# A fused attention and two-layer MoE kernel: the next-to-last gates issued ahead of the last products with v, and the last routing chain cut into other portions

## The chip, the cores and the metric

The kernel runs on one core of one Trainium2 chip, as one program. The metric is the device time of one execution in microseconds (us), taken as the median of several executions.

## The reference

Three stages follow each other. `attn_out` feeds the first MoE layer, whose result `x` feeds the second.

```python
mask = q_assign[:, :, :, None] == k_assign[:, :, None, :]   # same nearest centroid
attn = softmax(where(mask, scale * q @ k.T, -1e9)) @ v      # 2 batches, 8 heads, 768, 64
x = attn_out.transpose(0, 2, 1, 3).reshape(1536, 512)

logits = x @ w_gate                                         # layer 1: 8 experts
e = argmax(logits); gate = softmax(logits)[e]
y[i] = gate * relu(x[i] @ w1[e]) @ w2[e]                    # first `capacity` tokens of an expert

# layer 2: the same without capacity, times sigmoid(x @ w_output_gate)[e]
```

Each token goes to one expert. To know which token is in which place of which expert, a prefix count over all 1536 tokens is needed, so the full routing of layer 1 is known only after the last token has left attention.

## The kernel before, in words

**Attention.** The work is 8 pairs of heads (`pi` 0 to 7; two batches, four pairs each), and in each pair 12 steps (6 blocks of 128 queries, 2 heads). A step is: scores on TensorE (L238), row maximum on VectorE (L246), exponential on ScalarE (L254), and two steps later six transposes (L268) with evictions (L270). A "half" is three query blocks, 384 tokens; when a half of a pair is transposed, its products with v (`av`, 24 matmuls, L280) are issued and `av_out` copies them out on ScalarE (L287). `fin(pi, hf)` then calls `norm`: three matmuls `px` on TensorE turn the result back to tokens and give the partial gate logits (L299), VectorE takes reciprocals `ri` of the softmax sums (L301, L302), multiplies the logits into `lp` (L307), adds them up in `lg_sb` (L312, L313) and scales the rows of x (L315; by chunk L317 in the last half). All order of issue is written out by hand: each engine takes its instructions in the order in which this code emits them.

**Routing of a half.** After the fourth pair of a batch a half of tokens is complete, and the generator `after_half(b, hf, rows)` routes it: `choose` (five VectorE steps, L522 to L533), `sums` (three absolute sums of the last 128 columns on ScalarE, `jk`, L1430), `exps` (L1452 to L1454), `before` (running counts, L1436), `power` (a power of two to scale the rows by, L1441 and L669 to L673), `scale` (the rows themselves, 512 wide, one instruction per block; L1447 on ScalarE, L1449 on GpSimd), `gates` (L1457 to L1463) and `write` (rows to DRAM, `x1d`, L1467). `turns` issues several such chains round robin; `turns_by(k, ...)` does so k rounds at a time and yields between. The half that ends a batch goes on with `positions` (two matmuls, L1522), `places`, `load_order`, `taken`, and `invert`, which builds one-hot tables (`av` L587, `rv` L595) and multiplies them (`pinv`, L600). From that `select` makes the list of rows of an expert (L646, L649), and `gather` fetches them by indirect DMA on GpSimd (L867).

**The seam.** The last iteration of attention's loop (i = 97) calls, in this order, `fin(7, 0)`, both portions of `av(7, 1)` and `av_out(7, 1)`. `fin(7, 0)` only appends the steps of `after_half(1, 0)` to a list `bg`, which is emptied one step per iteration and fully after the loop; so those steps stand behind the last `av_out` in every queue. What is left, `norm` and `after_half` of half (7, 1), is the generator `last()`, handed to the MoE as a task.

**The head unit.** `M.run` works through units (one to three tiles of rows of one expert). Unit 0, the head, has 128 rows of an expert that the first batch already fixed, so it can run before the last routing is known. Per unit there are eight steps f of `mm1` (12 matmuls, L930; evicted by ScalarE `hh`, L932, then VectorE `hl`, L933) and four steps d of `mm2` (24 matmuls, L996; copied out by L998). `mm1` and `mm2` share one PSUM pool `ps_mm` of three buffers: a step can start only when the step three before it has been evicted. `SA` says how many portions of the routing task are issued ahead of each of the head's 12 steps, in the order f0 to f7, d0 to d3. Unit 1 begins with transposes `pxt` (L907) of gathered rows, which wait for the last routing. Weights of later units come over SyncE's queue (L791, L793), are split into two 16-bit parts by ScalarE (L820) and VectorE (L827), and multiplied three times.

Of the kernel before, what the change touches and what calls it, by code (L numbers as in the profile page):

```python
# [8 lines left out]
F32 = mybir.dt.float32  # L9
# [19 lines left out]
def attention(tc, end, ps_t, ident, wu, q, k, v, centroids, wg, x_half, lg_sb, consts, before_half, after_half, extra, slot):  # L29
# [13 lines left out]
    with ExitStack() as ctx:  # L43
# [239 lines left out]
        def av_out(pi, hf):  # L283
# [3 lines left out]
            nc.scalar.copy(ot, d["av", hf][:, :W])  # L287
            d["avo", hf] = ot

        def norm(pi, hf, by_chunk=False):  # L290
            b, hp = pairs[pi]
            d = st[pi]
            ot = d["avo", hf]
            c0 = hf * HALF
            t0 = b * C + c0
            px = ps_t.tile([P, 512], F32, tag="t", name="px")
            pv = px[:, :HALF * (P + 2 * E)].rearrange("p (c m) -> p c m", c=HALF)
            for c in range(HALF):
                nc.tensor.matmul(pv[:, c, :], ot[:, c * P:(c + 1) * P], rw[:, hp, :], start=True, stop=True)  # L299
            ri = end.tile([P, HALF, 2], F32, tag="ri", name="ri", bufs=2)  # L300
            nc.vector.tensor_scalar_add(ri, d["sm"][:, c0:c0 + HALF, :], 1e-9)  # L301
            nc.vector.reciprocal(ri, ri)  # L302
            rib = lambda n: ri.unsqueeze(3).to_broadcast([P, HALF, 2, n])
            xo = x_half(b, hf)[:, :, hp * P:(hp + 1) * P].rearrange("p c (j d) -> p c j d", j=2)
            lp = end.tile([P, HALF, 2, E], F32, tag="lp", name="lp", bufs=2)
            lo = lg_sb[:, t0:t0 + HALF, :]
            nc.vector.tensor_tensor(lp, pv[:, :, P:].rearrange("p c (j e) -> p c j e", j=2), rib(E), op=ALU.mult)  # L307
            if hp == 0:
                nc.gpsimd.tensor_tensor(lo, lp[:, :, 0], lp[:, :, 1], op=ALU.add)
            else:  # L310
                e = nc.vector if hp == NP - 1 else nc.gpsimd
                e.tensor_tensor(lo, lo, lp[:, :, 0], op=ALU.add)  # L312
                e.tensor_tensor(lo, lo, lp[:, :, 1], op=ALU.add)  # L313
            if not by_chunk:
                nc.vector.tensor_tensor(xo, pv[:, :, :P].rearrange("p c (j d) -> p c j d", j=2), rib(D), op=ALU.mult)  # L315
                return
            return [lambda c=c: nc.vector.tensor_tensor(xo[:, c], pv[:, c, :P].rearrange("p (j d) -> p j d", j=2),  # L317
                                                        ri[:, c].unsqueeze(2).to_broadcast([P, 2, D]), op=ALU.mult)
                    for c in range(HALF)]

        def fin(pi, hf):
            b, hp = pairs[pi]
            norm(pi, hf)
            if hp == NP - 2:
                bg.extend(before_half(b, hf))
            if hp == NP - 1:
                g = after_half(b, hf, ())
                bg.extend([lambda: next(g, None)] * (24 if hf else 8))

        def last():  # L330
            rows = norm(NPR - 1, 1, True)
# [142 lines left out]
def turns_by(k, *chains):  # L474

    chains = list(chains)
    while chains:
        for _ in range(k):
            chains = [c for c in chains if next(c, c) is not c]
        if chains:  # L480
            yield
# [225 lines left out]
class MoE:  # L707
# [23 lines left out]
    FX = 1  # L731
    FB = 2
    FY = 7
    SA = (1, 0, 1, 0, 1, 1, 0, 1, 1, 0, 1, 1)
    SB = (1, 3, 2, 1, 1, 1, 1, 1, 1, 1, 1, 1)
    Q = 2

# [539 lines left out]
def tile_kernel(tc, q, k, v, centroids, wg1, w11, w12, cap_in, wg2, wog2, w21, w22, out,  # L1277
# [15 lines left out]
    with ExitStack() as ctx:  # L1293
# [27 lines left out]
        if True:  # L1321
# [87 lines left out]
            def after_half(b, hf, rows):  # L1409
# [33 lines left out]
                    yield from R.power(rp, am, sx, rx)  # L1443

                def scale(i):
                    if end and i == 0:
                        nc.scalar.mul(x[:, i, :DM], x[:, i, :DM], sx[:, i:i + 1])  # L1447
                    else:
                        nc.gpsimd.tensor_scalar(x[:, i, :DM], x[:, i, :DM], sx[:, i:i + 1], None, op0=ALU.mult)  # L1449
# [72 lines left out]
                        nc.tensor.matmul(pp[:, i * E:(i + 1) * E], R.to[:, i], rs, start=True, stop=True)  # L1522
                    return pp

                yield from turns_by(1000 if end else 3, R.choose(rp, lg, None, oh1[:, t], mx), sums())
                if last:
                    rs = rp.tile([P, E], F16, tag="rs", name="rs")
                    with nc.allow_low_precision("whole numbers"):
# [2 lines left out]
                    vc = small("vc", C)  # L1531
                    lohi, ro = [], []
                if end:
                    yield
                    pp = positions()
                    exps()
                    yield from turns_by(KS, before(), power(), shift())
                    for i in range(HALF):
                        scale(i)
                    yield from turns_by(KS, places(), gates(), load_order())  # L1540
                    for i in range(HALF):
                        write(nc.scalar, slice(i, i + 1))
                    turns(taken())
                else:
                    yield
                    exps()
                    yield from turns_by(3, before(), power())
                    yield
                    for i in range(HALF):
                        scale(i)  # L1550
                    yield from turns_by(3, gates())
                    write(nc.sync, slice(0, HALF))
                    if not last:
                        return
                    yield
                    pp = positions()
                    yield from turns_by(3, places(), load_order())
                    yield from turns_by(3, taken())
# [343 lines left out]
```

## Time and profile before

| | |
|---|---|
| runs shown | 629.02, 629.38, 632.44 us; median 629.38 us |
| the profiled execution | 627.58 us, of which the span from first to last instruction is 625.7 us |
| TensorE (PE) busy | 569.5 us, 91% of the span |
| VectorE (DVE), ScalarE (ACT), GpSimd (POOL) busy | 467.1, 419.9, 212.8 us |
| mean granted TensorE clock | 0.976 of full speed |
| attention, head unit, rest of the MoE | to about 275, to 293, to 626 us |

Times on the trace are counted from the start of the span. A bracket at the end of a timeline row gives how long the engine had stood idle before that instruction and who ended the wait. PEclk is the granted clock of TensorE: 1.00 is 2.4 GHz, 0.50 is 1.2 GHz, and a value between them is a stretch with some of each. "ACTq" is a DMA issued from ScalarE's queue. A matmul's length in a row includes its way through the array, so lengths of following rows overlap; the distance between starts is the better measure.

### The profile page before, as it was taken

The page shows a single profiled execution, that of the slowest core. Times are in us where ns is not written, and L with a number is a line of the kernel's source. Part 1 is how long each engine was busy: PE and PEld are TensorE (multiplying, and loading weights), DVE is VectorE, ACT ScalarE, POOL GpSimd, SP SyncE. Part 2 cuts the span into 40 slices and gives each one's busy share as a digit, 9 for nine tenths or more (in the row PEclk, how much of TensorE's full clock was granted, in tenths as well). Part 3 has the DMA queues.
Part 4 walks back from the last instruction along what each step waited for, and adds up shares of the span by engine and source line. Part 5 has one row for each costly group of instructions (what it writes and reads, how often), then busy time and mean ns, then how long its engine had stood idle before and what let it go on. Part 6 is the DMA issues. An engine that isn't in the chain of part 4 may idle for free.

```text
span 625.7 us, 14519 instructions
## 1 busy us (share of the span) xinstructions
PE 569.5 (91%) x5430; PEld 470.8 (75%) x5430; DVE 467.1 (75%) x1219; ACT 419.9 (67%) x885; POOL 212.8 (34%) x420
## 2 busy tenths in 40 slices
PE   6899999998999988958999998998788899999992
PEld 2766767675767666637878997997767888999992
DVE  5767777679899677756597689788776566989881
ACT  4766666776666669832676776876654466979781
POOL 8702020204150210134615268344333623253341
PEclk9899999999999999998899999999899799999998
DMA  5779391826429952314486776977754457998930
GB/s 148 212 231 275 97 216 46 210 60 151 141 89 233 252 171 82 133 56 138 130 269 204 243 244 179 304 238 244 248 181 152 164 174 238 305 308 298 321 111 20
DMA packets 75518, 117.55 MB, mean 188 GB/s; under 512 B 10504, under 2 KB 43400, under 8 KB 75441
## 3 DMA queue, kind: packets, MB, share of 16 engines
q1 hardware_dynamic: 71585, 105.96, 56.1%
q0 software_dynamic: 3264, 9.72, 4.9%
q8 instruction: 45, 0.74, 0.5%
q10 hardware_dynamic: 592, 0.87, 0.4%
q14 instruction: 32, 0.26, 0.1%
HBM read 84.28 MB, written 12.87 MB: 155 GB/s over the span
## 4 chain that ended last, share of the span: by engine, by line
PE 63%; DVE 16%; ACT 9%; DMA 5%; issue 4%; SPq 1%; POOL 0%; ACTq 0%; DVEq 0%; POOLq 0%
PE ph L930 17%; PE py L996 13%; PE av L280 9%; PE pss L238 7%; PE ppt L268 6%; DVE wl L827 3%; DVE nm L246 3%; PE pz L971 3%; ACT pe L254 2%; PE pyo L1609 2%; PE pxt L907 2%; ACT pt L270 1%; ACT wh L820 1%; DMA xg<-x2d,idx2a 1%; DMA xg<-x2d,idx 1%
## 5 line engine op out<-in xcount | busy, mean ns | idle before, releaser
L827 DVE SCALAR_TENSOR_TENSOR wl<-raw,sw,wh 128x1024 f16<-128x1024 f32 x128 | 163.5, 1283 | 18.5 <-ACT wh L820 18.4
L820 ACT ACTIVATE wh<-raw,sw 128x1024 f16<-128x1024 f32 x128 | 145.7, 1146 | 2.6 <-DMA x<-ot 2.5
L246 DVE TENSOR_REDUCE nm<-pss 128x1 f32<-128x768 f32 x96 | 91.4, 952 | 40.5 <-PE pss L238 36.8
L254 ACT ACTIVATE pe<-pss,nm 128x768 f32<-128x768 f32 x96 | 87.1, 907 | 24.2 <-DVE nm L246 24.2
L930 PEld LDWEIGHTS <-wh 128*128 128x128 f16 x1152 | 91.3, 102 | 14.2 <-issue 9.7
L238 PE MATMUL pss<-y,x 128*128 128x384 f32 x384 | 93.5, 364 | 4.1 <-ACT pe L254 3.2
L268 PE MATMUL ppt<-ident,pe 128*128 128x128 f32 x576 | 80.5, 275 | 3.3 <-ACT pt L270 1.4
L238 PEld LDWEIGHTS pss<-y,x 128*128 128x128 f32 x384 | 63.0, 190 | 24.4 <-issue 12.3
L270 ACT COPY pt<-ppt 128x384 f32<-128x384 f32 x128 | 57.9, 482 | 28.6 <-PE ppt L268 28.2
L268 PEld LDWEIGHTS ppt<-ident,pe 128*128 128x128 f32 x576 | 69.3, 142 | 8.9 <-ACT pt L270 2.3
L930 PE MATMUL ph<-xh,wh 128*128 128x192 f16 (+14 forms) x576 | 69.5, 246 | 6.7 <-DVE hl L933 5.7
L996 PEld LDWEIGHTS <-wh 128*128 128x128 f16 x960 | 72.4, 99 | 3.8 <-issue 0.5
L930 PE MATMUL ph<-xl,wh 128*128 128x192 f16 (+14 forms) x576 | 69.5, 246 | 0.2
L930 PE MATMUL ph<-xh,wl 128*128 128x192 f16 (+14 forms) x576 | 69.5, 246 | 0.0
L280 PE MATMUL av<-pt,v 128*64 128x384 f32 x384 | 68.8, 494 | 0.0
L932 ACT ACTIVATE hh<-ph 128x128 f16<-128x128 f32 (+14 forms) x144 | 44.1, 312 | 35.7 <-PE ph L930 34.3
L933 DVE SCALAR_TENSOR_TENSOR hl<-ph,hh 128x128 f16<-128x128 f32 (+14 forms) x144 | 46.4, 333 | 24.6 <-ACT hh L932 24.0
L930 PEld LDWEIGHTS <-wl 128*128 128x128 f16 x576 | 47.4, 102 | 1.9
L996 PE MATMUL py<-hl,wh 128*128 128x192 f16 (+13 forms) x480 | 46.6, 239 | 0.8 <-DVE hl L933 0.8
L996 PE MATMUL py<-hh,wh 128*128 128x192 f16 (+13 forms) x480 | 46.5, 239 | 0.6 <-DVE hl L933 0.4
L280 PEld LDWEIGHTS av<-pt,v 128*64 128x64 f32 x384 | 24.8, 136 | 28.4 <-issue 28.2
L996 PE MATMUL py<-hh,wl 128*128 128x192 f16 (+13 forms) x480 | 46.1, 239 | 0.0
(319 smaller groups left out, 858.8 us busy)
## 6 DMA issues: line engine op xcount, KB each, us to landing
raw<-in_moe_w SPq DMA_DIRECT2D x64, 1024.0 KB, 5.9
y<-kh SPq DMA_DIRECT2D x31, 192.0 KB, 4.0
x<-qh SPq DMA_DIRECT2D x30, 192.0 KB, 4.2
q<-in_q SPq DMA_DIRECT2D x8, 384.0 KB, 5.1
k<-in_k SPq DMA_DIRECT2D x8, 384.0 KB, 5.3
x<-ql SPq DMA_DIRECT2D x16, 192.0 KB, 3.6
v<-in_v SPq DMA_DIRECT2D x8, 384.0 KB, 4.1
out<-zt SPq DMA_DIRECT2D x1, 3072.0 KB, 11.0
```

What stands on the lines that cost most here:

```text
L238: nc.tensor.matmul(p[:, hf, :W], xx[:, c * P:(c + 1) * P], yy[:, hf * W:(hf + 1) * W], start=a, stop=o)
L246: nc.vector.tensor_reduce(nm, p[:, :, :W], axis=AX.XY, op=ALU.max, negate=True)
L254: nc.scalar.activation(pe, p[:, :, :W], AF.Exp, bias=d["nm", c, j], scale=1.0, accum_out=d["sm"][:, c, j:j + 1])
L268: nc.tensor.transpose(p[:, kc * P:(kc + 1) * P], pe[:, kh, kc * P:(kc + 1) * P], ident)
L270: eng(pt[:, kh * HALF:(kh + 1) * HALF, (c % HALF) * P:(c % HALF + 1) * P], p.rearrange("p (a b) -> p a b", a=HALF))
L280: nc.tensor.matmul(p[j * D:(j + 1) * D, :W], d["v"][:, j, kc, :], d["pt", hf, j][:, kc, :], start=(kc == 0), stop=(kc == C - 1))
L820: nc.scalar.activation(hi[:, :, s], x[:, :, s], AF.Copy, scale=sw)
L827: nc.vector.scalar_tensor_tensor(lo[:, :, s], x[:, :, s], sw, hi[:, :, s], op0=ALU.mult, op1=ALU.subtract, accum_out=fl)
L930: nc.tensor.matmul(p[:, :N], w[:, c, fs], x[:, c, :N], start=(k == 0), stop=(k == 11))
L932: nc.scalar.activation(hh[:, f, :N], p[:, :N], AF.Relu)
L933: nc.vector.scalar_tensor_tensor(hl[:, f, :N], p[:, :N], 0.0, hh[:, f, :N], op0=ALU.max, op1=ALU.subtract)
L996: nc.tensor.matmul(p[:, :N], w[:, f, s], x[:, f, :N], start=(k == 0), stop=(k == 23))
```

## The change

Four things change. (1) When `fin` reaches the last pair (which it does for half 0 only), it empties `bg`, runs `after_half(1, 0)` to its end at once, and issues the reciprocals `ri` of half (7, 1) by the new function `inverse`; all that now stands ahead of the last `av` and `av_out` in the queues. (2) `norm` uses reciprocals that exist already. (3) `SA` is other: one portion ahead of each of f0 to f5, none ahead of f6 to d1, one ahead of d2 and of d3. (4) The chain of the last half is cut into other portions: `choose` and `sums` two rounds at a time instead of all at once; then `exps`, `power`, `before`, `shift` and `scale` in one portion; then a portion with nothing in it; then `positions`, `places`, `gates`, `load_order` and the writes in one; then `taken` and `invert`. Of the three `scale` instructions two are now ScalarE's, one GpSimd's (before: one and two).

Portion by portion (the step of the head unit that it is issued ahead of):

| | before | after |
|---|---|---|
| norm, all of choose and sums, `rs` | f0 | f0, f1, f2 (norm and two rounds; two rounds; the rest) |
| positions | f2 | f4 |
| exps, power, before, shift | f2, f4 | f2 |
| scale | f4 | f2 |
| places, gates, load_order | f4, f5, f7, d0 | f4 |
| writes, taken, invert tables | d0 | f4 (writes), f5 |
| pinv, select, gather | d2 | d2 |

```diff
--- before.py
+++ after.py
@@ -287,6 +287,14 @@
             nc.scalar.copy(ot, d["av", hf][:, :W])
             d["avo", hf] = ot
 
+        def inverse(pi, hf):
+
+            d = st[pi]
+            c0 = hf * HALF
+            ri = d["ri", hf] = end.tile([P, HALF, 2], F32, tag="ri", name="ri", bufs=2)
+            nc.vector.tensor_scalar_add(ri, d["sm"][:, c0:c0 + HALF, :], 1e-9)
+            nc.vector.reciprocal(ri, ri)
+
         def norm(pi, hf, by_chunk=False):
             b, hp = pairs[pi]
             d = st[pi]
@@ -297,9 +305,9 @@
             pv = px[:, :HALF * (P + 2 * E)].rearrange("p (c m) -> p c m", c=HALF)
             for c in range(HALF):
                 nc.tensor.matmul(pv[:, c, :], ot[:, c * P:(c + 1) * P], rw[:, hp, :], start=True, stop=True)
-            ri = end.tile([P, HALF, 2], F32, tag="ri", name="ri", bufs=2)
-            nc.vector.tensor_scalar_add(ri, d["sm"][:, c0:c0 + HALF, :], 1e-9)
-            nc.vector.reciprocal(ri, ri)
+            if ("ri", hf) not in d:
+                inverse(pi, hf)
+            ri = d["ri", hf]
             rib = lambda n: ri.unsqueeze(3).to_broadcast([P, HALF, 2, n])
             xo = x_half(b, hf)[:, :, hp * P:(hp + 1) * P].rearrange("p c (j d) -> p c j d", j=2)
             lp = end.tile([P, HALF, 2, E], F32, tag="lp", name="lp", bufs=2)
@@ -325,7 +333,15 @@
                 bg.extend(before_half(b, hf))
             if hp == NP - 1:
                 g = after_half(b, hf, ())
-                bg.extend([lambda: next(g, None)] * (24 if hf else 8))
+                if pi == NPR - 1:
+
+                    while bg:
+                        bg.pop(0)()
+                    for _ in g:
+                        pass
+                    inverse(pi, 1)
+                else:
+                    bg.extend([lambda: next(g, None)] * (24 if hf else 8))
 
         def last():
             rows = norm(NPR - 1, 1, True)
@@ -731,7 +747,7 @@
     FX = 1
     FB = 2
     FY = 7
-    SA = (1, 0, 1, 0, 1, 1, 0, 1, 1, 0, 1, 1)
+    SA = (1, 1, 1, 1, 1, 1, 0, 0, 0, 0, 1, 1)
     SB = (1, 3, 2, 1, 1, 1, 1, 1, 1, 1, 1, 1)
     Q = 2
 
@@ -1443,7 +1459,7 @@
                     yield from R.power(rp, am, sx, rx)
 
                 def scale(i):
-                    if end and i == 0:
+                    if end and i != 1:
                         nc.scalar.mul(x[:, i, :DM], x[:, i, :DM], sx[:, i:i + 1])
                     else:
                         nc.gpsimd.tensor_scalar(x[:, i, :DM], x[:, i, :DM], sx[:, i:i + 1], None, op0=ALU.mult)
@@ -1522,7 +1538,7 @@
                         nc.tensor.matmul(pp[:, i * E:(i + 1) * E], R.to[:, i], rs, start=True, stop=True)
                     return pp
 
-                yield from turns_by(1000 if end else 3, R.choose(rp, lg, None, oh1[:, t], mx), sums())
+                yield from turns_by(2 if end else 3, R.choose(rp, lg, None, oh1[:, t], mx), sums())
                 if last:
                     rs = rp.tile([P, E], F16, tag="rs", name="rs")
                     with nc.allow_low_precision("whole numbers"):
@@ -1531,15 +1547,17 @@
                     vc = small("vc", C)
                     lohi, ro = [], []
                 if end:
-                    yield
-                    pp = positions()
                     exps()
-                    yield from turns_by(KS, before(), power(), shift())
+                    turns(power(), before(), shift())
                     for i in range(HALF):
                         scale(i)
-                    yield from turns_by(KS, places(), gates(), load_order())
+                    yield
+                    yield
+                    pp = positions()
+                    turns(places(), gates(), load_order())
                     for i in range(HALF):
                         write(nc.scalar, slice(i, i + 1))
+                    yield
                     turns(taken())
                 else:
                     yield
```

## Rows read from the trace of the kernel before

**Rows 1.** The page's part 4: shares of the span on the chain that ended last

```profile
PE 63%; DVE 16%; ACT 9%; DMA 5%; issue 4%; SPq 1%; POOL 0%; ACTq 0%; DVEq 0%; POOLq 0%
```

**Rows 2.** The chain of 264 to 304 us: start, length, what

```profile
290.89 0.18 DVE idx L649
...
292.08 3.12 DMA xg<-x1d,idx
```

**Rows 3.** Timeline, 270 to 279 us: start, length, engine, line, [idle before <- releaser]

```profile
270.12 4.09 PE L280 MATMUL av<-pt,v 128*64 128x384 f32 x24
...
270.84 0.55 DVE L315 TENSOR_TENSOR x<-px,ri 128x384 f32<-128x384 f32 x1
...
274.26 0.48 ACT L287 COPY avo<-av 128x384 f32<-128x384 f32 x1 [4.36 <-PE av L280]
...
274.63 0.31 ACT L1430 ACTIVATE jk<-x 128x128 f16<-128x128 f32 x1
...
274.79 1.00 PE L299 MATMUL px<-rw,avo 128*128 128x144 f32 x6 [0.58 <-ACT avo L287]
...
275.94 0.16 DVE L1441 SCALAR_TENSOR_TENSOR am<-am 128x3 f32<-128x3 f32 x1 [3.32 <-ACT jk L1430]
...
276.69 4.68 POOL L1449 TENSOR_SCALAR x<-x,sx 128x512 f32<-128x512 f32 x3 [4.00 <-DVE sx L671]
...
277.72 0.58 DVE L301 TENSOR_SCALAR ri<-sm 128x6 f32<-128x6 f32 x1
...
278.65 0.21 DVE L307 TENSOR_TENSOR lp<-px,ri 128x48 f32<-128x48 f32 x1
...
278.90 0.18 DVE L312 TENSOR_TENSOR lg_sb<-lg_sb,lp 128x24 f32<-128x24 f32 x1
```

**Rows 4.** Timeline, 279 to 282 us: the last half's choice of experts

```profile
279.71 0.28 DVE L317 TENSOR_TENSOR x<-px,ri 128x128 f32<-128x128 f32 x1
...
279.80 0.31 ACT L1430 ACTIVATE jk<-x 128x128 f16<-128x128 f32 x1 [3.79 <-DVE er L525]
...
279.92 0.61 DVE L527 TENSOR_TENSOR er<-er,rev 128x24 f32<-128x24 f32 x1
...
281.36 0.21 PE L1522 MATMUL ppos<-rs,to 128*128 128x8 f16 x2 [4.22 <-DVE rs L1529]
```

**Rows 5.** Timeline, 282 to 286 us: the head unit beside the routing chain

```profile
282.72 0.28 ACT L932 ACTIVATE hh<-ph 128x128 f16<-128x128 f32 x1 [0.47 <-PE ph L930]
...
283.03 0.29 DVE L933 SCALAR_TENSOR_TENSOR hl<-ph,hh 128x128 f16<-128x128 f32 x1 [0.36 <-ACT hh L932]
...
284.18 0.71 ACT L1447 ACTIVATE x<-x,sx 128x512 f32<-128x512 f32 x1
...
284.60 0.17 DVE L1505 TENSOR_TENSOR pre<-pre,ppos 128x48 f32<-128x48 f32 x1
...
285.84 0.15 DVE L1463 TENSOR_TENSOR x<-rx,sm 128x3 f32<-128x3 f32 x1
```

**Rows 6.** Timeline, 287 to 296 us: from the writes to the next unit

```profile
287.35 1.35 ACTq L1467 DMA_DIRECT2D x1d<-x  x3
...
288.01 0.15 DVE L1511 TENSOR_SCALAR pl<-code 128x6 int32<-128x6 int32 x1
...
289.11 1.02 DVE L595 TENSOR_TENSOR rv<-lo,iota 128x384 f16<-128x384 int32 x2
...
290.27 0.61 PE L996 MATMUL py<-hh,wh 128*128 128x128 f16 x8
...
291.61 0.61 PE L996 MATMUL py<-hh,wh 128*128 128x128 f16 x8
...
295.33 0.66 PE L907 MATMUL pxt<-ident,xg 64*128 64x64 f32 x4 [2.22 <-DMA xg<-x1d,idx]
```

**Rows 7.** Stretches: length, busy us of PE, PEld, DVE, ACT, POOL (instructions), granted clock, DMA

```profile
281.40:285.10 3.70, 3.70 (x39) 3.70 (x40) 2.33 (x19) 1.54 (x5) 2.38 (x3) 0.54 0.56 222
295.30:302.10 6.80, 6.22 (x84) 5.99 (x85) 4.17 (x11) 5.09 (x11) 5.86 (x16) 0.50 0.30 89
455.70:462.50 6.80, 4.11 (x38) 3.38 (x36) 6.26 (x29) 4.94 (x12) 3.14 (x5) 1.00 0.63 211
```

More of the change, by code (lines that the diff above doesn't have):

```diff
@@ L1533, in after_half @@
                 if end:
+                    exps()
+                    turns(power(), before(), shift())
+                    for i in range(HALF):
+                        scale(i)
+                    yield
                     yield
                     pp = positions()
-                    exps()
-                    yield from turns_by(KS, before(), power(), shift())
-                    for i in range(HALF):
-                        scale(i)
-                    yield from turns_by(KS, places(), gates(), load_order())
+                    turns(places(), gates(), load_order())
                     for i in range(HALF):
                         write(nc.scalar, slice(i, i + 1))
+                    yield
                     turns(taken())
```

## The prediction

> **What bounds the kernel now.** I read the chain that ended last first: TensorE holds 63% of the span, VectorE 16% [rows 1]. For this change only the seam between attention and the first layer counts, so next came the chain there: the routing of the last half runs on VectorE until the index of unit 1's rows is out at 291.07 (290.89 + 0.18), the gather starts at 292.08 and lands 3.12 later [rows 2], and the transposes of unit 1, for which TensorE stood idle 2.22, start at 295.33 [rows 6]. What moves that transpose moves the end: behind it TensorE is the bound, and weight splits and loads are issued by the units, so they shift along. Then I read the timeline. ScalarE waits 4.36 for the products with v and only then does its sums `jk`; so VectorE waits 3.32 for them at `am`; so the last half's `lp` comes at 278.65, although its matmuls `px` were issued at 274.79 and took 1.00 [rows 3]. TensorE, after f0 and f1, waits 4.22 at the matmuls of `positions` [rows 4]. The windows show that it pays twice: from 281.4 to 285.1 its clock is 0.54 of full, and from 295.3 to 302.1 it is 0.50 [rows 7].
>
> **Part 1, the next-to-last gates ahead of the last products.** x of that half is ready at 271.4 (270.84 + 0.55). The three `jk` take 1.3 together (274.63 to `am` at 275.94) [rows 3], so `am` moves from 275.94 to 272.7. From `am` to `ri` 1.78 pass, from `ri` to the reciprocals' end 0.9 [rows 3]: all is done at 275.4, inside the products with v (4.09 from 270.12) and `px`. `av_out` is not delayed: ScalarE is free 1.3 before the products end at 274.2; without that margin every microsecond there would be one on `px`. So `lp` starts when `px` ends, about 275.9: **a lead of 2.75**. The write of that half goes to SyncE's queue about 3 earlier; nothing else stands in that queue then, so it neither costs nor gains. GpSimd's three scalings (4.68) move from 276.69 to 273.45, on an idle engine.
>
> **Part 2, choose in three portions.** Before, the whole choice ran ahead of f0's evictions; now f0's and f1's stand inside it. `jk` 0 starts 1.15 after `lp` [rows 3, 4]: 277.05. Behind `jk` 1 (0.43 later) ScalarE does `hh` 0 (0.28) at 277.8, VectorE then `hl` 0 (0.29) [rows 5], and the third step of the choice, which came 1.27 after `lp` [rows 3, 4], starts at 278.3 instead of 277.2. Then a row scaling (0.28 [rows 4]), `jk` 2, `hh` 1 and `hl` 1 lead to 279.65, and the tail of the choice ends at 280.0. Before, `positions` stood at 281.36: the lead is down to 1.3. TensorE waits in pieces now: for `hl` 0 ahead of f3, for the choice ahead of f4.
>
> **Part 3, two scalings on ScalarE.** `exps`, `power` and the counts are nine short VectorE steps about 0.1 apart, as the twelve between 284.60 and 285.84 are [rows 5], and end near 280.8. ScalarE then scales two blocks (0.71 each [rows 5]) ahead of `hh` 2 and `hh` 3, so `hl` 3 ends at 282.8. GpSimd's one scaling less is worth nothing, as GpSimd has no other work until the gather. `places` stands behind `hl` 3: 282.8 instead of 284.60, a lead of 1.8, since before it had waited there for f2 and f3 at the low clock.
>
> **Part 4, places to writes in one portion.** From `places` to the gate took 1.4 with one `hl` between [rows 5]; without it 1.1, to 283.9. The three writes wait for that gate at the head of ScalarE's queue and take 1.35 [rows 6]. Behind them stands `hh` 4, although f4 has long been computed: it ends at 285.5, `hl` 4 at 285.8, and f7, which needs that buffer, starts there. The writes, issued by 285.2 instead of 288.7, land earlier, but the gather waits for the index.
>
> **Part 5, taken and the tables ahead of `hl` 5.** They take 2.12 (288.01 to 289.11 + 1.02) [rows 6], so end at 287.9, and `hl` 5 at 288.2. `mm2`'s d0 reuses the buffer of f5: it starts at **288.2**. Two steps d take 2.68 at full clock (1.34 from 290.27 to 291.61 [rows 6]), and `pinv` stands behind d1: 290.9. Before, d1 was done just as the tables were, and the index started 0.76 after the tables' end; now all six small matmuls come after d1, some 0.2 more. Index at 291.6 to 291.9 instead of 290.89: **the lead of 2.75 is gone, and the gather lands 0.7 later.** I take 0.7; the bounds are 0 (VectorE's steps closer together than I set them) and 1.2 (one more slow step).
>
> **The clock.** By these steps TensorE between 277.6 and 288.2 works some 3.6 (f3 to f7, 0.67 each, half of a step d) and is idle some 7, in pieces of 0.7 to 1.9. No stretch of before has that pattern. Nearest are a fall at 295.3 after the 2.22 idle ahead of it, and a stretch without fall, 455.7 to 462.5, with 4.11 busy of 6.80 [rows 6, 7]. The idle share here is larger than in the second, so I take it that the clock falls to 1.2 GHz, for a stretch as that at 281.4 (3.7). The part of it that lies on waits costs nothing; on d0 and d1 it costs at most another 2.7. I take half, 1.35. In return unit 1's low stretch (6.8, in which at half clock 6.22 of work is worth 3.1) should come out shorter: between nothing and 1.55 back, I take 0.8.
> The Trainium skill ("TensorE: Matmul & The Clock Gate", section "A second HAM failure mode: psum-queue depth-cycling") describes this pattern: short idle pieces between groups, as PSUM buffers cycle, make the clock swing, and throughput suffers. It speaks against this change; by it the sum is this one or that of the second rival, while the stretch at 455.7 disagrees with it.
>
> **Sum.** 0.7 + 1.35 - 0.8 = +1.25 us against the profiled execution's 627.58: 628.8. That execution lies 1.8 under the median of 629.38; so the forecast for the median is **630.6**.
>
> **VectorE beside GpSimd.** While GpSimd scales (276.69 to 281.37), two VectorE steps took 0.58 and 0.61 where their like take 0.18 to 0.21; yet `lg`, with two inputs in SBUF, took 0.18 there [rows 3, 4]. So one step per GpSimd instruction pays some 0.4. After, the scalings lie at 273.45 to 278.1; two of three prices fall ahead of `px`'s end, the third on `lp` to the choice, instead of on its third step: no change.
> The Trainium skill ("SBUF — State Buffer", section "Who interferes with whom") says more: the shared port is held for a whole instruction, and a VectorE instruction with two SBUF inputs waits for it. `lg`'s 0.18 disagrees; what it would do here is the fourth rival.
>
> **The rivals.**
> First, the clock stays at 2.4 GHz through the head: +0.7, unit 1 as before, 630.1. The stretch at 455.7 speaks for it, the larger idle share against it. Chance 0.18.
> Second, **slower**: the clock falls before d0 begins and stays low through d1. It decides if the fall lies between some 284 and 288. Then d0 and d1 take 5.4 instead of 2.68, `pinv` moves by 2.7, and the idle time ahead of the gather lets unit 1 start low as before: +3.4, 632.8. For it: d0 waits for `hl` 5 after two idle pieces of 1.5 or so. Chance 0.17.
> Third, **faster**: evictions and tables interleave better than I hold, so that `places`' lead of 1.8 reaches the gather: 627.6; with the most that unit 1's clock gives back, 626.0. For it: the head's own work is under 11 (eight steps f of 0.67, four d of 1.34) and TensorE could end by 287. Against it: `hl` 5 behind the tables, `pinv` behind d1. Chance 0.10.
> Fourth, VectorE locked out: `lg` waits for the end of a scaling, its second step for the next (1.56 each, a third of 4.68 [rows 3]), and the choice begins after 278.1 instead of 276.6: 1.4 on top of +1.25, 632.0. Chance 0.08.
> Fifth, the change doesn't bring the gates forward, because a wait for all of the products with v stays in ScalarE's queue; the other portions then balance out: 629.4. Chance 0.04.
>
> **How the numbers follow.** The forecast has 0.43. Half a percent, 3.1 us, is about what a measurement of this kernel can tell from no change. Under 626.2 lie most of the third rival: 0.08. Over 632.5 lie the second rival and a bit of the fourth: 0.18. The rest, 0.74, is within. The range goes from 627.2, which takes in the third rival's first price, to 633.4, the second with 0.6 for the upper bound of part 5; some 0.07 is left out below, some 0.08 above.
>
> **What would show it.** Right: ScalarE's wait of 4.36 ahead of `av_out` gone or cut to 1.3, `lp` near 275.9, the writes issued from ScalarE's queue near 284, the first matmul `py` near 288, `pinv` straight behind d1, the index at 291.5 to 292, the granted clock low somewhere from 279 to 293. Wrong: `lp` later than 277; `py` starting before 287 or `pinv` waiting for the tables rather than for TensorE; the transposes of unit 1 before 294; or a seam as forecast and an end that doesn't follow it.

## The result, and the profile after

The changed kernel takes **633.37 us** (median of 20 runs, 629.94 to 636.77); the kernel before, run beside it, 629.19 us (20 runs, 625.21 to 635.38). The ratio is 1.006 with a 95% interval of 1.0038 to 1.0081, that is +3.8 us [2.4, 5.1]. The time is inside the range, but only 0.03 us under its top (633.4): a slowdown just over half a percent, where the forecast was no measurable change. By the time alone the second rival (632.8) was nearest.

The chain that ended last hardly differs on the page [rows 1]:

```profile
PE 61%; DVE 17%; ACT 10%; DMA 5%; issue 4%; POOL 1%; ACTq 0%; SPq 0%; DVEq 0%; POOLq 0%
```

The spans of the two profiled executions, 625.7 and 630.3 us, can't be compared as they stand. The last products with v start at 270.12 in one and at 274.16 in the other, although the instructions up to there are the same. These 4.0 us arise ahead of the seam; the changed kernel's two other profiles start there at 271.5 and 274.8 (below). So **from here on times are counted from the start of the last products with v**, except in rows, and "+10.14" means 10.14 us after it.

The timeline of the changed kernel through the seam (start, length, engine, line, [idle before <- releaser]; a line number is up to 16 higher than the same line's before):

```profile
274.16 4.09 PE L280 MATMUL av<-pt,v 128*64 128x384 f32 x24
...
276.83 0.16 DVE L1457 SCALAR_TENSOR_TENSOR am<-am 128x3 f32<-128x3 f32 x1 [0.17 <-ACT jk L1446]
...
278.29 0.48 ACT L287 COPY avo<-av 128x384 f32<-128x384 f32 x1 [1.38 <-PE av L280]
...
279.92 0.21 DVE L315 TENSOR_TENSOR lp<-px,ri 128x48 f32<-128x48 f32 x1 [0.51 <-PE px L307]
...
282.52 0.17 DVE L543 TENSOR_TENSOR er<-er,rev 128x24 f32<-128x24 f32 x1
...
284.30 0.20 PE L1538 MATMUL ppos<-rs,to 128*128 128x8 f16 x2 [0.81 <-DVE rs L1545]
...
284.96 1.33 ACT L1463 ACTIVATE x<-x,sx 128x512 f32<-128x512 f32 x2 [0.38 <-DVE sx L687]
...
286.83 0.38 PE L946 MATMUL ph<-xh,wh 128*128 128x128 f16 x4 [1.64 <-DVE hl L949]
286.90 0.20 DVE L1521 TENSOR_TENSOR pre<-pre,ppos 128x48 f32<-128x48 f32 x1
...
287.81 0.15 DVE L1479 TENSOR_TENSOR x<-rx,sm 128x3 f32<-128x3 f32 x1
...
288.07 1.35 ACTq L1483 DMA_DIRECT2D x1d<-x  x3
...
289.47 0.61 ACT L948 ACTIVATE hh<-ph 128x128 f16<-128x128 f32 x3 [2.85 <-DVE cnt L1494]
...
290.12 0.38 PE L946 MATMUL ph<-xh,wh 128*128 128x128 f16 x4 [1.79 <-DVE hl L949]
...
291.09 1.02 DVE L611 TENSOR_TENSOR rv<-lo,iota 128x384 f16<-128x384 int32 x2
...
292.02 0.68 DVE L949 SCALAR_TENSOR_TENSOR hl<-ph,hh 128x128 f16<-128x128 f32 x3
...
292.36 1.00 PE L1012 MATMUL py<-hh,wh 128*128 128x128 f16 x8 [1.41 <-DVE hl L949]
...
294.86 1.06 PE L1012 MATMUL py<-hh,wh 128*128 128x128 f16 x8
...
296.67 0.30 PE L616 MATMUL pinv<-av,rv 128*128 128x24 f16 x6
297.44 0.18 DVE L665 TENSOR_REDUCE idx<-w 128x3 int32<-128x24 f32 x1
...
301.62 0.43 PE L923 MATMUL pxt<-ident,xg 64*128 64x64 f32 x4 [1.96 <-DMA xg<-x1d,idx]
```

ScalarE's wait of 4.36 ahead of `av_out` [rows 3] is cut to 1.38, and `lp` comes 2.77 earlier, at +5.76 instead of +8.53 (278.65 - 270.12). But the idle times in TensorE's brackets behind it are new: 1.64 ahead of f5, 1.79 ahead of f7, 1.41 ahead of d0, in place of one of 4.22 [rows 4]. Three pieces of the routing chain make them. The two scalings hold ScalarE from 284.96 until `hh` 2 at 286.2, so that one, and with it f5, comes late. The writes wait for the last gate (287.81 + 0.15) and then hold ScalarE for 1.35, so ScalarE takes up `hh` 4 only after 2.85 without work, and f7 comes late. The tables hold VectorE until 292.11, so `hl` 5, and with it d0, comes late. And d0 itself takes 2.50 (294.86 - 292.36) where a step d took 1.34 before [rows 6] (its own d0 1.48, from 287.06 to 288.54): the clock. `pinv`, behind d1, is at +22.51; before it was at +19.76.

The waits of the same stretch, 279.6 to 302 us, say it in sums (us in total, times, longest):

```profile
PE ph L946 <- DVE hl L949: 4.3, 3, 1.8
...
ACT hh L948 <- DVE cnt L1494: 2.8, 1, 2.8
```

The windows say what TensorE did before its clock fell and after (columns as in [rows 7]):

```profile
285.30:292.36 7.06, 2.33 (x36) 2.09 (x36) 5.22 (x31) 2.22 (x8) 1.36 (x1) 1.00 0.32 116
292.36:296.70 4.34, 4.34 (x50) 4.34 (x50) 0.34 (x2) 0.27 (x1) 0.00 (x0) 0.61 0.00 0
```

From f5 to d0 it was busy 2.33 of 7.06, at full clock, with no idle piece longer than 1.8; then, busy all the time, it ran d0 and d1 at a clock of 0.61 on average, 1.2 GHz through d0 and the first half of d1. In this profile the low clock fell on work, not on waits.

### The profile page after: what moved, and what is told of

It reads as the page before. It is cut to its first block, busy times and chain, and to the rows that moved or that the text cites. A ratio compares the mean times of both kernels' runs of the same rounds, so it can differ in the third digit from the quotient of the medians.

```text
span 630.3 us, 14520 instructions
## 1 busy us (share of the span) xinstructions
PE 572.2 (91%) x5430; PEld 470.1 (75%) x5430; DVE 468.4 (74%) x1219; ACT 419.9 (67%) x886; POOL 209.6 (33%) x419
## 4 chain that ended last, share of the span: by engine, by line
PE 61%; DVE 17%; ACT 10%; DMA 5%; issue 4%; POOL 1%; ACTq 0%; SPq 0%; DVEq 0%; POOLq 0%
PE ph L946 16%; PE py L1012 12%; PE av L280 9%; PE pss L238 7%; PE ppt L268 6%; DVE wl L843 3%; DVE nm L246 3%; PE pz L987 2%; ACT pe L254 2%; PE pyo L1627 2%; PE pxt L923 2%; ACT wh L836 2%; ACT pt L270 1%; PE plog L153 1%; DMA out<-xo,tk 1%
## 5 line engine op out<-in xcount | busy, mean ns | idle before, releaser
L946 PE MATMUL ph<-xh,wh 128*128 128x192 f16 (+14 forms) x576 | 68.6, 243 | 11.2 <-DVE hl L949 10.2
```

What stands on the lines that cost most here:

```text
L946: nc.tensor.matmul(p[:, :N], w[:, c, fs], x[:, c, :N], start=(k == 0), stop=(k == 11))
```

## The experiments

One table holds the seam in all runs. Before, changed and their repeats show each of their three profiles. "Unit 2" is its first matmul, taken as the end of the seam; from there to the end of the kernel 314 to 319 us follow (means of three profiles: 317.3 before, 315.5 after). The ratio is to the kernel before on the same chip.

| kernel | positions | d0 | pinv | transposes | unit 2 | ratio, 95% interval |
|---|---|---|---|---|---|---|
| before | 11.24, 11.24, 11.24 | 16.94, 16.95, 17.94 | 19.76, 19.76, 20.75 | 25.21, 25.14, 26.21 | 38.57, 38.53, 38.40 | 1 |
| changed | 10.14, 10.14, 11.00 | 18.21, 18.19, 19.06 | 22.51, 23.26, 23.02 | 27.47, 28.34, 28.09 | 40.40, 40.68, 42.41 | 1.006 [1.0038, 1.0081] |
| e1 part 1 alone | 8.38 | 13.11 | 15.79 | 21.11 | 33.30 | 0.9949 [0.9915, 0.9982] |
| e2 portions alone | 12.70 | 20.76 | 24.76 | 29.65 | 41.83 | 1.006 [1.0029, 1.0091] |
| e3 tables at d0 | 10.14 | 16.62 | 19.43 | 24.39 | 36.58 | 0.9991 [0.9955, 1.0026] |
| e4 changed, filled | 10.14 | 18.20 | 20.88 | 25.75 | 38.01 | 1.001 [0.9975, 1.0044] |
| e7 before, filled | 11.99 | 16.89 | 19.57 | 24.92 | 37.13 | 0.9973 [0.9934, 1.0013] |
| e8 part 1, filled | 8.38 | 13.10 | 15.78 | 21.18 | 32.89 | 0.9921 [0.9885, 0.9957] |
| e11 choice at f0 | 8.39 | 20.65 | 16.46 | 26.79 | 39.13 | 1.0035 [0.9997, 1.0072] |
| e12 writes too at d0 | 10.14 | 16.14 | 18.95 | 24.39 | 36.64 | 1.000 [0.9969, 1.0031] |

**e1: part 1 alone.** The kernel before, with only the gates and reciprocals of part 1 moved (`inverse` and the use of its `ri` in `norm` as in the change, not shown); old `SA`, old portions.

```diff
                 g = after_half(b, hf, ())
-                bg.extend([lambda: next(g, None)] * (24 if hf else 8))
+                if pi == NPR - 1:
+
+                    while bg:
+                        bg.pop(0)()
+                    for _ in g:
+                        pass
+                    inverse(pi, 1)
+                else:
+                    bg.extend([lambda: next(g, None)] * (24 if hf else 8))
```

> The kernel before with part 1 alone: the next-to-last gates and the reciprocals go ahead of the last products with v, the last chain keeps its old portions. Theory A (the portions eat the lead; part 1 is worth its 2.75 us): lp starts as px ends, positions follow some 2.3 us earlier than before, f2 to f7 run without a long idle piece and at full clock, and the gather lands 2.5 to 4 us earlier than before, counted from the start of the last products; the median is 2.5 to 4 us under the kernel before. Rival B (part 1 is worth nothing, because TensorE's own work or the writes set when the gather starts): the gather lands where it did, within 0.7 us, and the median is within 1 us of the kernel before.

Positions came 2.86 earlier than before and the transposes 4.10 earlier; the median is 625.96 us (12 runs), -3.2 us [-5.3, -1.1] by the ratio. So part 1 is worth its lead, all of it, as theory A said (the transposes a little earlier than it said). In e1's timeline the tables and TensorE arrive together, and `pinv` waits only 0.23:

```profile
278.90 0.20 PE L1538 MATMUL ppos<-rs,to 128*128 128x8 f16 x2 [1.37 <-DVE rs L1545]
...
283.63 0.61 PE L1012 MATMUL py<-hh,wh 128*128 128x128 f16 x8 [0.49 <-DVE hl L949]
...
285.69 1.02 DVE L611 TENSOR_TENSOR rv<-lo,iota 128x384 f16<-128x384 int32 x2
...
286.77 0.24 PE L616 MATMUL pinv<-av,rv 128*128 128x24 f16 x3 [0.23 <-DVE rv L611]
...
287.48 0.18 DVE L665 TENSOR_REDUCE idx<-w 128x3 int32<-128x24 f32 x1
...
288.43 1.05 POOL L883 DMA_INDIRECT xg<-x1d,idx  x1 [4.77 <-DVE bw L672]
...
291.63 0.43 PE L923 MATMUL pxt<-ident,xg 64*128 64x64 f32 x4 [1.94 <-DMA xg<-x1d,idx]
```

**e2: the portions alone.** The changed kernel with `fin` as before.

```diff
-                if pi == NPR - 1:
...
-                else:
-                    bg.extend([lambda: next(g, None)] * (24 if hf else 8))
+                bg.extend([lambda: next(g, None)] * (24 if hf else 8))
```

> The changed kernel without part 1: the next-to-last gates stand behind the last av_out again, the last chain has the new portions. Theory A: the chain starts 2.75 us later than in the changed kernel and nothing catches it up, so the gather lands 2 to 3 us later than in the changed kernel, 4 to 5 us later than before; the median is 4 to 7 us over the kernel before. Rival B: the gather lands where the changed kernel's does, within 0.7 us, and the median is that of the changed kernel, 2.4 to 5 us over the kernel before.

The median, 633.43 us (12 runs), is that of the whole change, as rival B said, so by the medians alone part 1 adds nothing once the portions are changed. The seam of its one profile is later by 4.4 than before at the transposes, and by 1.3 to 2.2 than the changed kernel's three (theory A said 2 to 3); its clock is low for 13.65 us. Both kernels with the new portions are slow, so the portions are what costs; how much of part 1 is left beside them, the medians don't tell.

**e3: the tables ahead of d0 instead of f5.** One portion of the changed kernel moved.

```diff
-    SA = (1, 1, 1, 1, 1, 1, 0, 0, 0, 0, 1, 1)
+    SA = (1, 1, 1, 1, 1, 0, 0, 0, 1, 0, 1, 1)
```

> The changed kernel with one edit: taken and the one-hot tables are issued ahead of d0 instead of f5, so behind hl 5 to hl 7 on VectorE. Theory A (d0 waits for hl 5 behind the tables, pinv waits behind d1): the first py starts 1.2 to 1.8 us earlier than in the changed kernel, pinv waits for the tables instead of for TensorE and comes 1 to 3 us earlier; the median is 1 to 3 us under the changed kernel. Rival C (the low clock alone is the loss): the first py moves, but the tables end 0.9 to 1.5 us later, and pinv and the gather stay where they were within 0.7 us; the median is that of the changed kernel within 1 us.

d0 came 1.59 earlier and `pinv` 3.08, more than the tables hold VectorE, since the clock now stays full through d0 and d1. The median is 628.62 us: the whole slowdown is gone. In its timeline `hl` 5 no longer stands behind the tables, d0 follows f7 at once, and d0 takes 1.48 (291.46 to 292.94, the rows with each step's first 8 matmuls), as in the kernel before:

```profile
290.80 0.38 PE L946 MATMUL ph<-xh,wh 128*128 128x128 f16 x4 [1.78 <-DVE hl L949]
...
291.46 0.74 PE L1012 MATMUL py<-hh,wh 128*128 128x128 f16 x8
...
292.94 0.61 PE L1012 MATMUL py<-hh,wh 128*128 128x128 f16 x8
...
293.28 1.02 DVE L611 TENSOR_TENSOR rv<-lo,iota 128x384 f16<-128x384 int32 x2
...
294.28 0.32 PE L616 MATMUL pinv<-av,rv 128*128 128x24 f16 x6
...
295.07 0.18 DVE L665 TENSOR_REDUCE idx<-w 128x3 int32<-128x24 f32 x1
...
296.02 1.05 POOL L883 DMA_INDIRECT xg<-x1d,idx  x1 [8.68 <-DVE bw L672]
```

**e4: the changed order, the idle pieces filled.** Matmuls of zeros into a buffer that nobody reads, as many ahead of a step as its wait has room for; the order is that of the change.

```diff
+FILL = {3: 3, 4: 3, 5: 7, 7: 7, 8: 6}
...
+                if not prev and FILL.get(f):
+                    warm_up(self.nc, self.ps_g.tile([128, 512], F32, tag="g", name="fill"), self.wu, FILL[f])
```

> The changed kernel with matmuls of zeros into an unused PSUM tile in TensorE's idle pieces of the head: 3 of 128x512 ahead of f3, 3 ahead of positions, 7 ahead of f5, 7 ahead of f7, 6 ahead of d0 (0.22 us each at full clock; the pieces were 0.8, 0.8, 1.6, 1.8 and 1.4 us). The output is the same. Theory A with the clock as its second half: TensorE keeps 2.4 GHz through d1, d0 and d1 take 2.7 instead of 4.3 us, and the gather lands 1.3 to 1.8 us earlier than in the changed kernel; the median is 1 to 2 us under the changed kernel, still 0.5 to 2 us over the kernel before. Rival C (the low clock alone is the loss): the median falls to that of the kernel before or under it. Rival D (the clock costs nothing on the path): the gather lands where it did within 0.5 us.

d0 starts where it did in the changed kernel, at +18.20, so the order alone still makes it late; but the clock is full in the windows of f5 to d0 and of d0 and d1:

```profile
285.00:291.93 6.93, 6.40 (x56) 3.77 (x55) 5.23 (x31) 2.09 (x8) 1.23 (x1) 1.00 0.32 119
291.93:294.70 2.77, 2.77 (x52) 2.77 (x52) 0.34 (x2) 0.27 (x1) 0.00 (x0) 1.00 0.00 0
```

`pinv` comes 1.63 earlier than in the first changed profile, the transposes 1.72; against the first profile of before they are 0.54 late. The median is 629.73 us, 1.001 of before. So most of the loss is the clock, which falls with the idle pieces, and what the profile leaves to the order without it is about half a microsecond; whether it is that or nothing (rival C), the medians don't tell. That e3 and e4 each remove nearly all isn't a contradiction: the order makes the idle pieces, the clock falls on them, and the low stretch lands on d0 and d1. Taking out either link is enough. The fall is not certain, though. In e3 the pieces ahead of f5 and f7 are as long (1.64 and 1.78), and in its one profile the clock stayed full from f5 to d0:

```profile
285.98:291.46 5.48, 2.16 (x36) 2.04 (x36) 3.43 (x24) 1.94 (x7) 1.36 (x1) 1.00 0.36 134
```

**e5, e6, e9, e10: each kernel twice more.** Unchanged, one profile each, because the low stretches lay at other places than expected and the start of the seam at other times.

> The kernel before, unchanged, a second profile. Theory E (the profiled execution of before had an unlucky clock: its low stretch of 6.8 us began just as unit 1 did, while the changed kernel's profile had only 3.4 there; so the profiles show 1.8 us of loss from the last products to unit 2 where the medians show 4.2): the stretch from the start of the last products to unit 2's first matmul, 38.6 us in the first profile, comes out at 35.5 to 37. Rival F (the seam is always as in the first profile and the rest of the 4.2 is lost after unit 1): 38 to 39 again, and the stretch from unit 2 to the end shorter than 317.0 by 1 to 2 us.

> The changed kernel, unchanged, a second profile. Theory E: from the start of the last products to unit 2's first matmul 39.5 to 42 us (40.4 in the first profile), the first py 18.1 to 18.3 us after that start whatever the clock does. Rival F: 40 to 41, and the stretch from unit 2 to the end longer than 315.7 by 1 to 2 us.

> The kernel before, unchanged, a third profile. Theory H (a part of the measured 4.2 lies in attention, ahead of the change: in both profiles of the changed kernel the scores of the seventh pair, near 201 us, wait 1.0 and 1.4 us longer for the copies of the one-hot rows, which fly beside a weight load, than in both profiles of before): no such wait again, within 0.2 us of the first profile; last products to unit 2 38.5 us. Rival I (that wait comes and goes by chance): it shows here too, 0.3 us or more.

> The changed kernel, unchanged, a third profile. Theory H: the extra wait near 201 us shows again, 0.6 to 1.4 us. Rival I: it may be absent. Both: last products to unit 2 40 to 41 us.

The seam is no chance: up to unit 2 it took 38.40 to 38.57 in the three profiles of before and 40.40 to 42.41 in those of the changed kernel, 2.66 more in the mean (41.16 against 38.50). So theory E fell, and rival F had only the seam right: from unit 2 to the end e5 was longer (319.2) and e6 shorter (314.3), where it had expected the opposite. Unit 2 in e10, at 42.41, is later than either theory said. What varies beside the seam is the start: the last products began at 270.1, 270.3, 271.5 before and at 274.2, 271.5, 274.8 after. A wait for one-hot copies near 201 us, which might have come with the change (theory H), stood in a profile of before too (1.2 us longer in e9), as rival I said. Where the low clock falls is chance in part: in e6 it covered d0 and d1 whole,

```profile
289.66:295.00 5.34, 5.34 (x56) 5.34 (x56) 0.33 (x2) 0.30 (x2) 0.00 (x0) 0.50 0.00 0
```

in e10 it began at +11.55, ahead of f5, and lasted 10.2 us. In e10 the last products themselves began at half clock (0.50 in the first 1.3 us), so positions and d0 are 0.86 later there from the outset. The single times (629.76, 628.18, 627.51, 635.43 us) say nothing alone; 628.18 is even under the lowest of the changed kernel's 20 runs (629.94).

**e7: before, its one long wait filled.** Zero matmuls, issued as in e4, in the 4.22 that TensorE waits ahead of `positions` [rows 4].

```diff
+FILL = {2: 18}
```

> The kernel before with 18 matmuls of zeros (128x512, 0.22 us each at full clock, 3.9 together) into an unused PSUM tile ahead of positions, where TensorE stood idle 4.2 us. The output is the same. If the clock's fall after that wait is on the path (theory A's second half): f2 to f5 run 0.67 apart instead of 1.28, places start 1 to 1.8 us earlier, the gather lands 1 to 1.8 us earlier than in the first profile of before, and the median is 0.5 to 2 us under the kernel before. Rival D (the clock costs nothing on the path): the gather lands where it did within 0.5 us and the median is within 0.7 us of the kernel before.

f2 to f6 then start 0.67 apart, at full clock, where before f2 and f3 ran at half of it. The transposes are at +24.92, 0.3 earlier, with a start of f0 that was 0.76 later than before's in this profile; counted from f0 they are 1.1 earlier. Unit 2 is 1.44 earlier. The median of 627.34 us has 1 in its ratio's interval. Probably a gain, of at most 4 us; not shown.

**e8: e1, filled ahead of `positions` and of unit 1's transposes.**

```diff
+FILL = {2: 6, 12: 8}
```

> Part 1 alone, with 6 matmuls of zeros ahead of positions (1.4 us of idle time there) and 8 ahead of unit 1's transposes (1.9 us of idle time). The output is the same. If what is left of the clock's cost is on the path: no low stretch between the last products and unit 2, unit 2's first matmul 0.5 to 2 us earlier than with part 1 alone (33.3 us after the last products' start), and the median is 0.5 to 2 us under part 1 alone, 4 to 5 us under the kernel before. Rival G (unit 1 is bound by VectorE's splits, not by TensorE's clock): unit 2 starts where it did with part 1 alone, within 0.5 us, and the median is that of part 1 alone within 1 us.

There is no low stretch in the seam any more, but unit 2 starts only 0.41 earlier than in e1, within what rival G allowed. In e8's timeline TensorE, at full clock, waits within unit 1 for ScalarE and VectorE, 1.35 in four pieces up to its first `py`; before, at half clock, it waited there once, 0.46:

```profile
292.66 0.28 PE L947 MATMUL ph<-xh,wh 128*128 128x64 f16 x4 [0.46 <-ACT xh L925]
293.12 0.28 PE L947 MATMUL ph<-xl,wh 128*128 128x64 f16 x4 [0.18 <-DVE xl L926]
...
295.77 0.28 PE L947 MATMUL ph<-xh,wh 128*128 128x64 f16 x4 [0.35 <-DVE hl L950]
...
297.11 0.28 PE L947 MATMUL ph<-xh,wh 128*128 128x64 f16 x4 [0.36 <-DVE hl L950]
```

The median of 625.34 us (ratio 0.9921) is the lowest of all; its interval overlaps e1's, so the filling itself isn't shown to help.

**e11: the whole choice ahead of f0 again.**

```diff
-    SA = (1, 1, 1, 1, 1, 1, 0, 0, 0, 0, 1, 1)
+    SA = (1, 0, 1, 1, 1, 1, 0, 0, 0, 0, 1, 1)
...
-                yield from turns_by(2 if end else 3, R.choose(rp, lg, None, oh1[:, t], mx), sums())
+                yield from turns_by(1000 if end else 3, R.choose(rp, lg, None, oh1[:, t], mx), sums())
```

> The changed kernel with the choice of experts whole ahead of f0 again (the other portions, and the steps they stand at from f2 on, as changed; none at f1). Theory A with the prediction's terms: the choice is no longer behind hl 0 and hl 1, so positions come 0.8 to 1.5 us earlier than in the changed kernel (10.1 us after the last products' start), places 0.8 to 1.3 earlier than its 12.7, d0 0.8 to 1.3 earlier than its 18.2; the median is 0.5 to 2 us under the changed kernel. Rival J (hl 2 and hl 3 behind the two scalings on ScalarE decide, wherever the choice stands): places and d0 stay within 0.4 us.

The expectation missed, and the edit did more than meant: without a pause inside the choice, the powers and the scalings went ahead of f0 as well, and all later portions moved one step forward. It shows the other side of the balance. The index was 5.6 us earlier, but f3 and `pinv`, which now stands ahead of f5, waited in TensorE's timeline

```profile
282.44 0.58 PE L946 MATMUL ph<-xh,wh 128*128 128x128 f16 x4 [2.43 <-DVE hl L949]
...
287.88 0.24 PE L616 MATMUL pinv<-av,rv 128*128 128x24 f16 x3 [2.72 <-DVE rv L611]
```

and the head unit ended only near +26.8, so unit 1's rows lay waiting. Part of that lateness is the clock: f3 to f7 ran mostly at half of it (rows of 0.63 instead of 0.39). Routing that is early by holding the head back is worth nothing: the transposes need both.

**e12: e3, and the writes too ahead of d0.**

```diff
+                    yield
                     for i in range(HALF):
                         write(nc.scalar, slice(i, i + 1))
-                    yield
                     turns(taken())
```

> The changed kernel with both the writes and taken with the tables issued ahead of d0. Against the kernel with the tables alone at d0 it undoes what holds hh 4 behind three writes on ScalarE (part 4). Theory A with the prediction's terms: hh 4 is done as f4 ends, so hl 4 waits only for load_order's end, f7 starts 0.4 to 0.8 us earlier than its 16.0 us, d0 0.3 to 0.8 us earlier than the 16.6 with the tables alone at d0, and pinv, which waits for the tables, 0.2 to 0.8 us earlier than 19.4; the median is within 1 us of that kernel. Rival K (the writes decide more than the tables): the gain is 1.3 us or more. Rival L: the writes, issued later, land after the index is ready and the gather comes later than with the tables alone at d0.

f7, d0 and `pinv` came 0.48 earlier, as expected: the writes no longer held `hh` 4. The transposes didn't move at all (+24.39 in both). In the timeline the index is out at 294.29, but the gather starts 1.24 later, where e3 had 0.77 (295.25 to 296.02):

```profile
290.79 1.35 ACTq L1483 DMA_DIRECT2D x1d<-x  x3
...
294.11 0.18 DVE L665 TENSOR_REDUCE idx<-w 128x3 int32<-128x24 f32 x1
...
295.53 1.05 POOL L883 DMA_INDIRECT xg<-x1d,idx  x1 [8.65 <-DVE ov L676]
```

The gather reads what the writes store, and all profiles together show that it waits for them. In ten of the fourteen it starts 0.77 after the index. In the other four it starts later, 0.98 to 1.01 in the three of before and 1.24 here, and in these four it starts 3.36 to 3.39 after the issue of the last write has ended (here 292.14, in the first profile of before 288.70 [rows 6]). No run tried this wait by itself.

## Why the prediction was right or wrong

**The order was right, step by step.** From the start of the last products: `lp` forecast +5.8, measured +5.76; third step of the choice +8.2, +8.36; positions +9.9, +10.14; places +12.7, +12.74; writes issued +15.1, +15.26; tables' end +17.8, +17.95; d0 +18.1, +18.21. `pinv` at full clock was forecast at +20.8 and is at +20.88 in e4. The 0.7 for the gather without the clock is 0.54 there at the transposes (25.75 against 25.21), and 0.23 against the mean of before's three profiles (25.52). One small term was left out: before, the gather waited some 0.24 for its last write (e12), so the earlier writes were not worth nothing. That the lead of 2.75 is spent within the portions, on hl 0 behind the choice, `hh` 4 behind the writes and `hl` 5 behind the tables, holds.

**The step that failed is "The clock", in both of its terms.** It let the clock fall, rightly, and its busy and idle shares were near (4.05 busy of 10.52 measured from f2's end to d0; the items it lists add up to 4.0, not 3.6). But it took half of 2.7 for d0 and d1, and no row stood behind the half. From d0 to `pinv` the changed kernel took 4.30, 5.07 and 3.96 in its three profiles, e4 at full clock 2.68: a price of 1.62, 2.39 and 1.28, in the mean 1.8 instead of 1.35. In the first two the idle pieces come first and the fall follows them, so the low stretch lies on the busy steps behind. In e10 the clock was low from f5 on, and there the prediction's sentence on waits held: from positions to d0 it took 8.06, against 8.07 in the first profile. At the transposes the three profiles are 1.72, 2.59 and 2.34 behind e4, 2.2 in the mean; 0.86 of e10's share comes from the slow start of its last products.

**The 0.8 that unit 1 should give back did not come.** From the transposes to unit 2 the changed kernel took 12.93, 12.34 and 14.32, before 13.36, 13.39 and 12.19: a mean of 13.20 against 12.98. A shorter low stretch is worth something: with 6.8 us of it in unit 1 it took 13.36 and 13.39, with 3.4 us 12.18 to 12.34 in eight profiles, with none 11.71 (e8) and 12.34 (e11). But before's third profile had the short one as well, the changed kernel's third had two of 3.4 us, and in its first and third TensorE waited 0.6 longer for ScalarE near the end of unit 1 (0.78 and 0.76 instead of 0.17).

Put right, the sum is 0.2 + 2.2 + 0.2 = 2.6 by the profiles, and the seams give 2.66; the measured interval, 2.4 to 5.1, takes both in. What the middle of that interval has over them, about 1 us, stays open: it would have to lie in the 270 us ahead of the seam or the 315 behind it, where profiles of one kernel differ by more than that. One trace of it may be the start. The first scores came at 12.6 to 13.4 us in all six profiles with the old portions (before, e1, e7, e8), and at 13.7 to 16.0 in six of the eight with the new ones, although the instructions up to there are the same; the other two, e6 and e11, came at 12.6 and 12.8. Whether the change has a hand in that, no run here shows.

That the time still fell inside the range is luck in part: the range's top was set by the second rival, and the seams account for 2.66 of the measured 3.8.

The Trainium skill ("TensorE: Matmul & The Clock Gate", section "A second HAM failure mode: psum-queue depth-cycling") describes short idle pieces between groups that make the clock swing; the prediction set the stretch at 455.7 [rows 7] against it. The changed kernel sides with the Trainium skill: with 2.33 busy of 7.06 in short pieces the clock fell, with the pieces filled (6.40 of 6.93) it did not. The stretch at 455.7, 4.11 busy of 6.80 without a fall, was no guide to this one; and e3, 2.16 busy of 5.48, shows that the fall can also stay away.

**The rivals.** The first (clock stays full) is what e4 makes of the kernel, not what the change does. The second, slower, was nearest by the time. Its condition was a fall between 284 and 288 by before's times; here the falls came at +18.25, +17.0 and +11.55, that is 288.4, 287.1 and 281.7, so it was met once, in e6, and there its price of 2.7 was nearly paid (2.39). The third, faster, fell with the new portions: the transposes came 2.3 to 3.1 later, not earlier. With the old portions part 1 is faster (e1). There its lead of 2.75 even grew to 4.1: the wait ahead of `positions` was shorter (1.37 instead of 4.22), f2 and f3 ran at full clock, and the gather no longer waited for the last write. The fourth fell: `lg` took 0.18 at 280.16, in the middle of GpSimd's scalings (277.58 to 282.26), and the choice was on time. So did the fifth, by ScalarE's wait of 1.38.

## What to carry to other kernels

Move work out from behind a long wait first, alone, and measure it: here the few lines of e1 beat both kernels (ratio 0.9949), and the rearrangement around them took the gain away and more. When a chain on slower engines is interleaved with matmuls, count for each portion which eviction stands behind it in its queue; several short waits of TensorE in place of one long one can cost its clock on the busy work that follows, so price that as a range up to the whole of that work at half speed (here 1.3 to 2.4 of 2.7 us were lost), not as a half. Then ask whether both inputs of the next unit, its index and the free engine, arrive together: in e11 being early with one was worth nothing.

## What was not expected of the hardware

The same program showed a low clock of other lengths at the same place, 3.4 us in one profile of the changed kernel, 6.8 in the next, 10.2 in the third; and of before 3.4, 3.4 and 6.8. A single profile of a stretch with short waits is one draw.

The 270 us ahead of the change, the same instructions in the same order, took 270.1 to 274.8 us. One source is the kernel's start: in the first changed profile pairs of matmuls near 8 us start 0.63 apart, where before they start 0.32 apart, and the first scores come at 16.02 instead of 12.61. The granted clock reads 1.00 there in both, so by the spacing TensorE ran at half speed where that record doesn't show it. Another source is the wait near 201 us. Ten to twelve runs of a kernel left intervals of 0.3 to 0.4% to either side; smaller differences need more runs, or a stretch counted from a mark inside the trace.

An indirect gather began 0.77 us after its index was out, but never less than 3.36 us after the issue of the last write to the rows it reads had ended (fourteen profiles; in four of them, before's three and e12, the write decided).
